# Another order of the first batch's weight rounding and of the weight loads, in a kernel of linear attention and a feed-forward layer

## The chip, the cores and the metric

The kernel runs on one core of one Trainium2 chip. The metric is device microseconds of one execution, median of three. The core has five engines with queues of their own, each strictly in order: PE (matrix products; its weight loads are listed apart as PEld), DVE (vector), ACT (scalar functions), POOL (general) and SP, which here only issues DMA transfers. PE writes into PSUM, of which there are eight banks of 128x512 float32; the rest lies in SBUF.

## The reference

```python
# q, k, v: (8, 8, 576, 64) float32; w_in (512, 2048) and w_out (2048, 512) float64
q_s = exp(q - q.max(-1)); q_s /= q_s.sum(-1) + 1e-9
k_s = exp(k - k.max(2));  k_s /= k_s.sum(2) + 1e-9       # over the sequence
kv = einsum('bhsd,bhse->bhde', k_s, v)
attn = einsum('bhsd,bhde->bhse', q_s, kv)
x = attn.transpose(0, 2, 1, 3).reshape(4608, 512)
out = relu(x @ w_in) ** 2 @ w_out
```

The weights come in 8 bytes per element. The kernel reads them as two 32-bit words and rounds them to float32 itself; float32 numbers are then split into a high and a low part, and each product is made of three (high x high, low x high, high x low).

## The kernel before

**Tiling.** Attention is done per batch and pair of heads: 8 batches of 4 pairs. A pair yields x for 512 of the 576 tokens of its batch in one of four column chunks (`x_hi`, `x_lo`); the other 64 tokens of every batch go to DRAM (`x_left`) and form a ninth block. The feed-forward layer does nine blocks of 512 tokens; in each it makes 16 steps, one per chunk `fc` of 128 hidden columns. A step has a hidden part (`ffn_h`, or `h_part` for the first four: 4 column chunks x 3 matmuls of 128x512, L406 to L408), an activation (`activate`: relu on ACT, square on DVE, `g_hi` on ACT, `g_lo` on POOL or DVE) and, two steps later, an output part (`ffn_out`: 4 x 3 matmuls, L440 to L442), so 24 matmuls a step.

**Weights.** `load_w` fetches a chunk of w_in ("i0" to "i15") or w_out ("o0" to "o15"), 512 KB each, through SP's queue. `split_weight` rounds it: ACT makes a small number of the top byte (L164, here "low word") and scales the upper word into PSUM bank 3 (L166, "bank row"), DVE joins them in two operations (L168, L169, giving `w`), then `finish_split` makes the high part on ACT (L176, a cast) and the low part on POOL (L177). Bank 3 is the only one for this, so ACT's next bank row waits until DVE has made the `w` before it. A low word is ordered behind the last entry of the list `his`.

**Attention of a pair.** `k_max` (DVE maximum, PE transposition L222, DVE `mc`, PE product L250), `k_exp` (`ke`), `q_exp` (DVE row maximum `qm`, POOL subtraction, ACT exp), `q_norm`, `kv` (PE, then `rs` on DVE and `kvn` on DVE or ACT), transposition of q, and the product that gives x (L358), split into `x_hi` (ACT, L188) and `x_lo` (DVE, L189).

**Order.** The program is one long list of instructions; a scheduler lays out each engine's queue by priority and data, units of attention in the first part ranking above the weights' rounding. In the first batch the four pairs run three units apart; behind the fifth unit of each pair one weight chunk is rounded, and behind its eighth the hidden parts of the first four chunks `hs` get this pair's share. After that the steps of block 0 run with attention of batch 1 spread among them in slots (`FIRST_KV`, `EARLY_STEP`, `EARLY_AT`). Two sets of buffers for k, q and v are used in turn, so the third pair's load needs the first pair's tile to be free. At most eight transfers of SP are outstanding. In block 0 the chunks are taken in the order `order0`: 2, 3, 0, 1, 4, 5, ...

Of the kernel before, what the change touches and what calls it, by code (L numbers as in the profile page):

```python
# [8 lines left out]
F32 = mybir.dt.float32  # L9
# [7 lines left out]
P = 128  # L17
# [5 lines left out]
half = slice(0, HALF), slice(HALF, P)  # L23
FLT_MAX = float.fromhex("0x1.fffffep127")
RAWB, WB = 4, 3
EARLY_SPLITS = [("o",2),("o",3),("i",4),("o",0)]
OFFSET = 100
AHEAD = 4
EARLY = 8
PRE = 4  # L30
LOADS = "k0 q0 v0 k1 q1 v1 k2 q2 w0 v2 k3 q3 v3 w1 w2 w3".split()
# [11 lines left out]
def attention_ffn_kernel(ctx: ExitStack, tc: tile.TileContext, q, k, v, w_in, w_out, out):  # L43
# [73 lines left out]
    def load(dst, src, b, pr, n):  # L117
        s = src[b, 2 * pr : 2 * pr + 2]
        lo = s[:, :SPLIT, :].rearrange("h (p j) d -> p h j d", j=LOW)
        hi = s[:, SPLIT:, :].rearrange("h (p j) d -> p h j d", j=HIGH)  # L120
        if n < 2 or b == 0:
            e = nc.scalar if (b, pr, n) in ACT_LOADS else nc.sync
            e.dma_start(dst[:HALF], lo)  # L123
            e.dma_start(dst[HALF:, :, :HIGH, :], hi)
        else:
            for h in range(2):
                nc.sync.dma_start(dst[:HALF, h, :, :D], lo[:, h])
                nc.sync.dma_start(dst[HALF:, h, :HIGH, :D], hi[:, h])

    def tiles(b, pr):  # L130
        i = pr if b == 0 else pr % NB
# [6 lines left out]
        for n in range(3):  # L138
            load_one(b, pr, n)

    chunks, last = [], []

    def load_w(part, fc):
        raw = stay.tile([P, 512, 2], U32, name=f"raw_{part}{fc}", tag=f"{part}{fc}")
# [33 lines left out]

        unsplit.append(parts)

    his, unsplit = [], []

    def finish_split():
        while unsplit:
            unsplit.pop()()

    def split(hi, lo, src):
        nc.scalar.copy(hi, src)  # L188
        nc.vector.tensor_tensor(lo, src, hi.bitcast(F32), op=ALU.subtract)  # L189

    def ordered(f, *args):
# [286 lines left out]
    us = [attention(0, pr) for pr in range(NPAIR)]  # L478
    for u in us:
        u[5], u[6] = u[6], u[5]  # L480
    hs = [banks[i] if i < 2 else ps_first.tile([P, NT], F32, name=f"h_ps{i}", tag="h") for i in range(PRE)]
    for c in LOADS:
        i = int(c[1])
        if c[0] == "w":
            load_w("i", i)
        else:
            load_one(0, i, "kqv".index(c[0]))
    order0 = list(range(2, PRE)) + list(range(min(2, PRE))) + list(range(PRE, NFC))

    def load_more(n):  # L490
        load_w("o", order0[n])
# [5 lines left out]
    for t in range(len(us[0]) + SKEW * (NPAIR - 1)):  # L497
        for pr in range(NPAIR):
            n = t - SKEW * pr
            if 0 <= n < len(us[pr]):  # L500
                with tc.high_priority(OFFSET):
                    us[pr][n]()
                if n == 4:
                    split_weight("i", pr)
                    if pr == NPAIR - 1:
                        for c in EARLY_SPLITS:
                            split_weight(*c)
                if n == 7:
                    finish_split()
                    for fc in range(min(PRE, pr + 1)):  # L510
                        for cc in [pr] if fc < pr else range(pr + 1):
                            h_part(hs[fc], 0, fc, cc)
    start.close()
    ps_o = ctx.enter_context(tc.tile_pool(name="ps_o", bufs=4, space=bass.MemoryType.PSUM))
    late = ctx.enter_context(tc.tile_pool(name="late", bufs=1))
    x_hi.append(late.tile([P, NCC, NT], F32R, name="x_hi1"))
# [1 line left out]

    for pr in range(NB):
        load_pair(1, pr)  # L520
    for n in range(AHEAD, NFC):
        load_more(n)
    steps = [(0, fc) for fc in order0] + [(blk, fc) for blk in range(1, B + 1) for fc in range(NFC)]
    LAG = 2
# [3 lines left out]
    for b in range(1, B):  # L528
        for pr in range(NPAIR):
            if b == 1:  # L530
                base, offs = FIRST_KV + EARLY_STEP * pr, EARLY_AT
            else:
                base, offs = 2 * NFC * (b - 1) + 1 + STEADY_STEP * pr, STEADY_AT
            us = attention(b, pr)
            nxt = b * NPAIR + pr + NB
            if nxt < B * NPAIR:
                i = 5 if b == 1 else 4
                us[i] = lambda f=us[i], nxt=nxt: (f(), load_pair(nxt // NPAIR, nxt % NPAIR))
            for u, o in zip(us, offs):
                slots.setdefault(base + o, []).append(u)  # L540
    for cc, u in enumerate(left_units()):
        slots.setdefault(2 * NFC * (B - 1) + 4 + 6 * cc, []).append(u)


    def in_slot(i):
        for u in slots.get(i, []):
# [60 lines left out]
```

## Time and profile before

| | us |
|---|---|
| median of 3 runs (lowest, highest) | 905.96 (905.91, 908.08) |
| profiled execution, whole | 906.89 |
| its span | 905.0 |
| PE busy | 875.9 (97%) |
| DVE busy | 580.8 (64%) |
| ACT busy | 408.1 (45%) |
| POOL busy | 202.1 (22%) |

The profile is of one execution. Times in it count from the start of the span. Busy PE means that matmuls were in flight, not that it ran at its peak, and the granted clock (1.00 is full) has to be read with it: at half clock PE is just as busy and does half as much. A row of the engines' order of time gives start, duration, engine, line, operation, output and inputs, and in brackets the idle time before it with what ended it. A wait is shown as who waited, for whom, microseconds in total, times, longest.

### The profile page before, as it was taken

To read this page: it belongs to the slowest core of one execution; us is meant where nothing else is said; L and a number is where in the kernel's file an instruction comes from. 1 tells how busy PE (TensorE), PEld (TensorE's weight loads), DVE (VectorE), ACT (ScalarE), POOL (GpSimd) and SP (SyncE) were. 2 spreads that over 40 slices of the span, in tenths; PEclk is the share of its full clock that TensorE was granted. 3 is DMA by queue.
4 is the path that set the end of the run, shared out by engine and by line. 5 is a ranking of instruction groups with operands and counts; after the bars stand their busy time and mean duration, and the time that the engine had idled before them with its cause. 6 is when DMAs were issued, how large, how long until landed. Compare 5 with 4: busy or idle time off the path is not lost.

```text
span 905.0 us, 12673 instructions
## 1 busy us (share of the span) xinstructions
PE 875.9 (97%) x4368; PEld 702.4 (78%) x4368; DVE 580.8 (64%) x1177; ACT 408.1 (45%) x801; POOL 202.1 (22%) x177
## 2 busy tenths in 40 slices
PE   4898989999999999999999999999999999999997
PEld 3576767888878888888888888888888888888885
DVE  6767887887778776878688768876764342222222
ACT  3766756545445443454454444444444232222222
POOL 3666635222213210222122212222222000000000
PEclk9989999999999999999999999999999999999999
DMA  9898211422142223322322123222311030002001
GB/s 234 274 324 246 62 35 54 114 77 82 46 117 71 78 64 89 97 72 71 86 80 81 54 76 96 76 65 65 97 31 32 3 93 1 1 1 46 1 1 46
DMA packets 95743, 73.18 MB, mean 81 GB/s; under 512 B 47552, under 2 KB 85440, under 8 KB 95680
## 3 DMA queue, kind: packets, MB, share of 16 engines
q1 hardware_dynamic: 94944, 71.53, 28.7%
q10 hardware_dynamic: 736, 0.85, 0.4%
q8 instruction: 34, 0.56, 0.2%
q14 instruction: 29, 0.24, 0.1%
HBM read 54.00 MB, written 18.35 MB: 80 GB/s over the span
## 4 chain that ended last, share of the span: by engine, by line
PE 85%; DMA 7%; DVE 4%; SPq 2%; issue 1%; ACT 0%; DVEq 0%
PE bank L406 14%; PE o_ps L440 14%; PE bank L407 14%; PE bank L408 14%; PE o_ps L441 14%; PE o_ps L442 13%; DMA qt<-in_q_dram 4%; DMA raw_i<-in_moe_w_in_dram 3%; PE bank L299 2%; PE bank L378 1%; DMA kt<-in_k_dram 1%; DVE w L169 1%; SPq L149 1%; DVE m L237 1%; SPq L123 0%
## 5 line engine op out<-in xcount | busy, mean ns | idle before, releaser
L406 PE MATMUL bank<-x_hi,wi 128*128 128x512 f32 x568 | 227.6, 401 | 4.3 <-ACT x_hi L188 2.2
L440 PE MATMUL o_ps<-wo,g_hi 128*128 128x512 f32 x576 | 227.5, 397 | 0.8 <-ACT g_hi L419 0.8
L441 PE MATMUL o_ps<-wo,g_hi 128*128 128x512 f32 x576 | 225.7, 392 | 0.0
L407 PE MATMUL bank<-x_lo,wi 128*128 128x512 f32 x568 | 225.6, 397 | 0.0
L408 PE MATMUL bank<-x_hi,wi 128*128 128x512 f32 x568 | 225.2, 396 | 0.0
L442 PE MATMUL o_ps<-wo,g_lo 128*128 128x512 f32 x576 | 224.1, 391 | 0.0
L418 DVE TENSOR_TENSOR r<-r 128x512 f32<-128x512 f32 x128 | 112.0, 875 | 123.3 <-ACT r L412 123.0
L423 DVE TENSOR_TENSOR g_lo<-r,g_hi 128x512 fp32r<-128x512 f32 x132 | 99.3, 752 | 105.8 <-ACT g_hi L419 104.1
L419 ACT CAST g_hi<-r 128x512 fp32r<-128x512 f32 x144 | 89.2, 620 | 129.1 <-PE o_ps L441 77.2
L412 ACT ACTIVATE r<-bank 128x512 f32<-128x512 f32 x142 | 84.5, 596 | 106.1 <-PE bank L408 103.4
L406 PEld LDWEIGHTS bank<-x_hi,wi 128*128 128x128 f32 x568 | 107.6, 190 | 30.9 <-ACT x_hi L188 3.6
L440 PEld LDWEIGHTS o_ps<-wo,g_hi 128*128 128x128 f32 x576 | 108.1, 188 | 25.7 <-ACT g_hi L419 1.0
L408 PEld LDWEIGHTS bank<-x_hi,wi 128*128 128x128 f32 x568 | 107.7, 190 | 24.3
L442 PEld LDWEIGHTS o_ps<-wo,g_lo 128*128 128x128 f32 x576 | 108.1, 188 | 22.9
L441 PEld LDWEIGHTS o_ps<-wo,g_hi 128*128 128x128 f32 x576 | 108.1, 188 | 22.9 <-POOL wo L177 0.2
L407 PEld LDWEIGHTS bank<-x_lo,wi 128*128 128x128 f32 x568 | 107.5, 189 | 22.8 <-issue 0.2
L389 POOL TENSOR_TENSOR x_lo<-xf,x_hi 128x256 fp32r<-128x256 f32 x48 | 39.5, 823 | 378.2 <-ACT x_hi L388 377.4
L332 POOL TENSOR_TENSOR qs<-qT,qs 64x640 fp32r<-64x640 f32 x48 | 81.7, 1703 | 58.7 <-ACT qs L331 50.9
L218 DVE TENSOR_REDUCE m<-kt 128x128 f32<-128x640 f32 x32 | 41.4, 1296 | 18.3 <-DMA kt<-in_k_dram 18.3
L331 ACT CAST qs<-qT 64x640 fp32r<-64x640 f32 x48 | 34.8, 726 | 37.9 <-DMA qT<-bounce 37.4
L380 ACT COPY xf<-bank 64x320 f32<-64x320 f32 (+1 forms) x96 | 37.9, 395 | 22.5 <-PE bank L378 14.3
L265 ACT ACTIVATE qn<-qn 128x640 f32<-128x640 f32 x32 | 23.6, 739 | 53.8 <-DVE qn L262 44.9
(118 smaller groups left out, 775.8 us busy)
## 6 DMA issues: line engine op xcount, KB each, us to landing
out_dram<-o SPq DMA_DIRECT2D x70, 128.0 KB, 2.4
raw_i<-in_moe_w_in_dram SPq DMA_DIRECT2D x16, 512.0 KB, 9.3
raw_o<-in_moe_w_out_dram SPq DMA_DIRECT2D x16, 512.0 KB, 9.0
bounce<-tb SPq DMA_DIRECT2D x24, 320.0 KB, 2.2
qT<-bounce SPq DMA_DIRECT2D x96, 80.0 KB, 2.3
kt<-in_k_dram SPq DMA_DIRECT2D x32, 160.0 KB, 3.0
qt<-in_q_dram SPq DMA_DIRECT2D x30, 160.0 KB, 3.0
vt<-in_v_dram SPq DMA_DIRECT2D x56, 80.0 KB, 2.5
```

The costliest lines, as they stand in the source:

```text
L218: nc.vector.tensor_reduce(m, kk.rearrange("p h j d -> p h d j"), axis=AX.X, op=ALU.max)
L332: nc.gpsimd.tensor_tensor(qs[other], qT[own], qs[own].bitcast(F32), op=ALU.subtract)
L406: nc.tensor.matmul(ps, wi[fc][:, 0, sl], xh[:, cc, :], start=(cc == 0), stop=False)
L407: nc.tensor.matmul(ps, wi[fc][:, 0, sl], xl[:, cc, :], start=False, stop=False)
L408: last.append(nc.tensor.matmul(ps, wi[fc][:, 1, sl], xh[:, cc, :], start=False, stop=(cc == NCC - 1)))
L412: nc.scalar.activation(r, ps, AF.Relu)
L418: nc.vector.tensor_tensor(r, r, r, op=ALU.mult)
L419: gh = nc.scalar.copy(g_hi, r)
L423: e.tensor_tensor(g_lo, r, g_hi.bitcast(F32), op=ALU.subtract)
L440: nc.tensor.matmul(acc[t], g_hi[:, ts], wo[fc][:, 0], start=(n == 0), stop=False)
L441: nc.tensor.matmul(acc[t], g_hi[:, ts], wo[fc][:, 1], start=False, stop=False)
L442: prev = nc.tensor.matmul(acc[t], g_lo[:, ts], wo[fc][:, 0], start=False, stop=(n == NFC - 1))
```

## The change

In the first batch only the first two hidden chunks (`BESIDE = 2`) are rounded and multiplied beside attention, one behind the fifth unit of each of the first two pairs. i2, o0, i3 and o1 are rounded in the program behind the attention of the batch, and the hidden parts of chunks 2 and 3 follow as a whole; a list `start_done` and an entry of each first-batch `x_hi` into `his` order their low words behind the `x_hi` issued last. Before, i2, i3, o2, o3, i4 and o0 were rounded in that stage, the last four in one go behind the fourth pair's kv. The steps of block 0 are taken in plain order 0, 1, 2, ...; the PSUM tiles of the first four hidden parts are swapped to match. Of the weights loaded after the start, o4 to o7 and i8 to i11 are issued behind the loads of batch 1's first two pairs as before; o8 to o11 and i12 to i15 are ordered behind the last v load of the third pair, o12 to o15 behind that of the fourth.

```diff
-EARLY_SPLITS = [("o",2),("o",3),("i",4),("o",0)]
+
+BESIDE = 2
+EARLY_SPLITS = [("i",2),("o",0),("i",3),("o",1)]
 OFFSET = 100
 AHEAD = 4
+
+LATER = 8, 12, 16
...
             for h in range(2):
                 nc.sync.dma_start(dst[:HALF, h, :, :D], lo[:, h])
-                nc.sync.dma_start(dst[HALF:, h, :HIGH, :D], hi[:, h])
+                dmas.append(nc.sync.dma_start(dst[HALF:, h, :HIGH, :D], hi[:, h]))
...
-    chunks, last = [], []
+    chunks, last, dmas = [], [], []
...
-    his, unsplit = [], []
+    his, unsplit, start_done = [], [], []
...
     def split(hi, lo, src):
-        nc.scalar.copy(hi, src)
+        c = nc.scalar.copy(hi, src)
+        if not start_done:
+            his.append(c)
         nc.vector.tensor_tensor(lo, src, hi.bitcast(F32), op=ALU.subtract)
...
-    hs = [banks[i] if i < 2 else ps_first.tile([P, NT], F32, name=f"h_ps{i}", tag="h") for i in range(PRE)]
+    hs = [ps_first.tile([P, NT], F32, name=f"h_ps{i}", tag="h") if i < 2 else banks[i - 2] for i in range(PRE)]
...
-    order0 = list(range(2, PRE)) + list(range(min(2, PRE))) + list(range(PRE, NFC))
+    order0 = list(range(NFC))
...
-                if n == 4:
+                if n == 4 and pr < BESIDE:
                     split_weight("i", pr)
-                    if pr == NPAIR - 1:
-                        for c in EARLY_SPLITS:
-                            split_weight(*c)
                 if n == 7:
                     finish_split()
-                    for fc in range(min(PRE, pr + 1)):
-                        for cc in [pr] if fc < pr else range(pr + 1):
-                            h_part(hs[fc], 0, fc, cc)
+                    for fc in range(BESIDE):
+                        if fc <= pr:
+                            for cc in [pr] if fc < pr else range(pr + 1):
+                                h_part(hs[fc], 0, fc, cc)
+    for c in EARLY_SPLITS:
+        split_weight(*c)
+    finish_split()
+    for fc in range(BESIDE, PRE):
+        for cc in range(NCC):
+            h_part(hs[fc], 0, fc, cc)
     start.close()
+    start_done.append(1)
...
-    for n in range(AHEAD, NFC):
+    for n in range(AHEAD, LATER[0]):
         load_more(n)
...
-                us[i] = lambda f=us[i], nxt=nxt: (f(), load_pair(nxt // NPAIR, nxt % NPAIR))
+                us[i] = lambda f=us[i], nxt=nxt: (f(), load_next(nxt))
...
+    def load_next(nxt):
+        load_pair(nxt // NPAIR, nxt % NPAIR)
+        i = nxt - NPAIR - NB
+        if i + 1 < len(LATER):
+            with tc.issue_after(dmas[-1].ins):
+                for n in range(LATER[i], LATER[i + 1]):
+                    load_more(n)
```

The rows below give an engine's queue. A row has the line, the operation, output<-inputs with buffer numbers and the shape; lines of the change are 4 to 6 higher than those of before (L164 is L168, L166 is L170, L176 is L180, L188 is L192, L224 is L230).

ACT, at the end of the first batch's attention. `raw_` names a weight chunk, `bank3` the bank of the rounding. Before, from the copies of the transposed q of the last two pairs to the last `x_hi`:

```order
L352 COPY qT_91<-bank2_88 128x512
L352 COPY qe_502<-first_ps_503 128x512
L166 ACTIVATE bank3_89<-raw_o3_168 128x512
L176 CAST wo2_473<-w_466 128x512
L164 ACTIVATE raw_i4_166<-raw_i4_166 128x512
L352 COPY qe_502<-first_ps_509 128x64
L352 COPY qT_91<-bank2_88 128x64
L188 CAST x_hi0_75<-first_ps_512 128x512
L166 ACTIVATE bank3_89<-raw_i4_166 128x512
L176 CAST wo3_481<-w_474 128x512
L164 ACTIVATE raw_o0_172<-raw_o0_172 128x512
L188 CAST x_hi0_75<-bank2_88 128x512
```

The same place now, from the last pair's kvn to the next batch's first exp:

```order
L319 ACTIVATE kvn1_85<-first_ps_417,rs_438 64x64 x2
L358 COPY qe_447<-first_ps_454 128x64
L358 COPY qT_91<-bank2_88 128x512
L192 CAST x_hi0_75<-first_ps_457 128x512
L168 ACTIVATE raw_i2_160<-raw_i2_160 128x512
L168 ACTIVATE raw_o0_164<-raw_o0_164 128x512
L358 COPY qT_91<-bank2_88 128x64
L192 CAST x_hi0_75<-bank2_88 128x512
L170 ACTIVATE bank3_89<-raw_o0_164 128x512
L180 CAST wi2_477<-w_472 128x512
L168 ACTIVATE raw_i3_162<-raw_i3_162 128x512
L271 ACTIVATE qn_618<-qn_618 128x640
```

Between the two `x_hi`, and ahead of them, fewer rows of rounding stand; the rows of i2, o0 and i3 follow behind the last `x_hi`.

DVE, at the first key product of batch 1 (`mc` is its maximum, which PE needs ahead of the first output step; `r` is the square of the activation). Before:

```order
L272 TENSOR_REDUCE qs_824<-qn_758 128x10
L224 TENSOR_REDUCE mc_648<-bank2_88 128x1
L416 TENSOR_TENSOR r_610<-r_610,h_ps2_130 128x512
L416 TENSOR_TENSOR r_617<-r_617,h_ps3_131 128x512
L255 TENSOR_TENSOR ke_674<-kt0_78,bank2_88 128x640
L274 RECIPROCAL qs_824<-qs_824 128x10
```

Now:

```order
L422 TENSOR_TENSOR r_626<-r_626,bank0_86 128x512
L280 RECIPROCAL qs_816<-qs_816 128x10
L172 SCALAR_TENSOR_TENSOR bank3_89<-bank3_89,raw_i4_166 128x512
L173 SCALAR_TENSOR_TENSOR w_577<-raw_i4_166,bank3_89 128x512
L172 SCALAR_TENSOR_TENSOR bank3_89<-bank3_89,raw_o2_172 128x512
L230 TENSOR_REDUCE mc_624<-bank2_88 128x1
L173 SCALAR_TENSOR_TENSOR w_583<-raw_o2_172,bank3_89 128x512
L422 TENSOR_TENSOR r_674<-r_674,bank1_87 128x512
L261 TENSOR_TENSOR ke_650<-kt0_78,bank2_88 128x640
L266 TENSOR_REDUCE qm_941<-qt0_82 128x10
```

`mc` stands behind three squares and the rounding of i4 and half of that of o2, where before it stood ahead of the first square, two rows behind the rounding of o0.

SP, the loads of batch 1's third and fourth pair (`qt0`, `kt0`, `vt0`: third pair; `qt1`: fourth). Before:

```order
L123 DMA qt0_82<-in_q_dram 64x2x320
L147 DMA raw_i14_596<-in_moe_w_in_dram 128x4x256
L124 DMA qt0_82<-in_q_dram 64x2x256
L367 DMA x_left_77<-left_499 128x64
L367 DMA x_left_77<-left_541 128x64
L149 DMA raw_o11_598<-in_moe_w_out_dram 128x1024
L147 DMA raw_i15_600<-in_moe_w_in_dram 128x4x256
L149 DMA raw_o12_602<-in_moe_w_out_dram 128x1024
L149 DMA raw_o13_604<-in_moe_w_out_dram 128x1024
L149 DMA raw_o14_606<-in_moe_w_out_dram 128x1024
L149 DMA raw_o15_608<-in_moe_w_out_dram 128x1024
L123 DMA qt1_83<-in_q_dram 64x2x320
```

Now:

```order
L151 DMA raw_i11_568<-in_moe_w_in_dram 128x4x256
L127 DMA qt0_82<-in_q_dram 64x2x320
L128 DMA qt0_82<-in_q_dram 64x2x256
L373 DMA x_left_77<-left_444 128x64
L373 DMA x_left_77<-left_469 128x64
L127 DMA qt1_83<-in_q_dram 64x2x320
L128 DMA qt1_83<-in_q_dram 64x2x256
L127 DMA kt0_78<-in_k_dram 64x2x320
L128 DMA kt0_78<-in_k_dram 64x2x256
L132 DMA vt0_80<-in_v_dram 64x4x64
L131 DMA vt0_80<-in_v_dram 64x5x64 x2
L132 DMA vt0_80<-in_v_dram 64x4x64
```

Both q loads stand directly behind i11, with nothing of o8 and later ahead of them; o8 is the next row behind these, and the fourth pair's k (`kt1`) follows i15.

## The prediction, as written before the run

> **What bounds the kernel now.** I read the page first (engine shares, chain), then the engines by stretch, PE's waits, the chain in order of time, and the engines' rows from 35 to 60 us.
>
> ```profile
> span 905.0 us, 12673 instructions
> PE 85%; DMA 7%; DVE 4%; SPq 2%; issue 1%; ACT 0%; DVEq 0%
> ...
> 55.77:82.40 26.63, 26.63 (x149) 20.58 (x149) 18.66 (x36) 22.00 (x42) 19.39 (x17) 1.00 1.07 332
> 82.60:86.00 3.40, 0.23 (x2) 0.23 (x3) 2.58 (x3) 2.51 (x6) 2.88 (x3) 1.00 0.47 126
> 86.00:89.40 3.40, 3.40 (x10) 2.69 (x10) 3.26 (x5) 0.56 (x1) 0.60 (x1) 0.52 0.60 154
> 96.50:133.10 36.60, 33.07 (x174) 24.25 (x172) 33.89 (x77) 23.24 (x46) 17.29 (x14) 1.00 0.17 44
> 133.10:600.00 466.90, 466.86 (x2375) 378.08 (x2376) 358.27 (x759) 224.36 (x452) 108.06 (x85) 1.00 0.29 79
> ```
>
> After the stretch come its length, then PE, PE's weight loads, DVE, ACT, POOL, the granted clock, DMA share and GB/s. From 133.1 us on PE is never idle and its work is unchanged, so the end moves only as much as PE's place at 133 us moves. Ahead of that there are three stages. Up to 55.77 PE waits for the first x and weights. From 55.77 to 82.40 it is full. Then it stands, runs at half clock, and to 133 us shares the bound with DVE (33.89 of 36.60 us busy), losing 36.60 - 33.07 = 3.5 us.
>
> ```profile
> PE bank L222 <- DVE m L218: 3.3, 1, 3.3
> PE bank L406 <- DVE r L416: 2.1, 3, 1.2
> PE bank L222 <- ACT kvn L313: 0.8, 1, 0.8
> PE bank L299 <- DVE x_lo L189: 0.7, 1, 0.7
> ...
> 60.76 11.31 DMA qt<-in_q_dram
> 73.16 9.88 DMA qt<-in_q_dram
> 83.13 0.62 DVE qm L260
> 84.54 1.18 DVE m L218
> 86.39 0.43 PE bank L407
> 89.98 0.23 PE bank L407
> 91.14 0.04 DVE ke L255
> 93.61 2.82 DMA kt<-in_k_dram
> ```
>
> The longest of PE's waits, 3.3 us, is the key maximum of the second batch's third pair. DVE had queued it behind a row maximum of q (83.13), and that q took 9.88 us to land behind weights of far later steps. The wait also cost clock: a half-rate matmul follows the last after 0.43 us, a full one after 0.23, so 3.4 us at half rate lose 3.4 x 0.20 / 0.43 = 1.6. The stall is worth 3.3 + 1.6 = 4.9 us.
>
> **The change: the later weights.** On SP's queue the two q loads of the third and fourth pair, and the third pair's k, now stand behind i11; o8 to i15 come after the third pair's v, o12 to o15 after the fourth's. Nothing is added: 16 + 16 weight issues before and after. The eight weights that stay ahead of q move 8 x 0.512 = 4.2 MB. At the 332 GB/s of the full stretch that is 12.6 us from their first issue:
>
> ```profile
> 45.97 0.59 SPq L149 DMA_DIRECT2D raw_o<-in_moe_w_out_dram  x1
> ...
> 39.59 1.29 DVE L218 TENSOR_REDUCE m<-kt 128x128 f32<-128x640 f32 x1
> 40.79 0.69 DVE L169 SCALAR_TENSOR_TENSOR w<-raw_o,bank 128x512 uint32<-128x512 uint32 x1
> 41.38 0.82 DVE L260 TENSOR_REDUCE qm<-qt 128x10 f32<-128x640 f32 x1
> 54.14 0.29 DVE L224 TENSOR_REDUCE mc<-bank 128x1 f32<-128x128 f32 x1 [2.44 <-PE bank L222]
> ...
> 54.49 0.49 PE L250 MATMUL bank<-ident,mc 128*128 128x128 f32 x2 [0.38 <-DVE mc L224]
> 55.77 0.47 PE L440 MATMUL o_ps<-wo,g_hi 128*128 128x512 f32 x1 [0.80 <-ACT g_hi L419]
> ```
>
> So q lands near 59 to 61 us, third k (which waits for the first pair's subtraction to free its buffer) near 63, 20 us ahead of PE's need. The stall of 3.3 us and the half clock behind it go: **-4.9**. Late weights: o8 is issued after the second batch's first kv, near 68, and rounded near 85. The fourth pair's k queues behind o8 to i15, 68 + 12.6 = 80.6; DVE reaches it behind the second kv, near 82. Covered, by some 1.5 us: cost nothing.
>
> **The change: rounding in the first batch.** On ACT, between the last pair's kvn and the last x_hi, two of seven rounding rows are left; a low word, two bank rows and two casts are gone:
>
> ```profile
> 48.08 1.26 POOL L262 TENSOR_TENSOR qn<-qt,qm 128x640 f32<-128x640 f32 x1
> 49.75 1.28 POOL L177 TENSOR_TENSOR wo<-w,wo 128x512 fp32r<-128x512 f32 x1
> ...
> 43.14 0.57 ACT L188 CAST x_hi<-bank 128x512 fp32r<-128x512 f32 x1
> ...
> 56.18 0.66 ACT L164 ACTIVATE raw_i<-raw_i 128x512 uint32<-128x512 uint8 x1
> 56.75 0.66 ACT L164 ACTIVATE raw_o<-raw_o 128x512 uint32<-128x512 uint8 x1
> 57.30 0.72 ACT L256 ACTIVATE ke<-ke 128x640 f32<-128x640 f32 x1
> 57.93 1.07 ACT L412 ACTIVATE r<-bank 128x512 f32<-128x512 f32 x2
> 58.89 0.65 ACT L166 ACTIVATE bank<-raw_o 128x512 f32<-128x512 f32 x1
> 59.44 0.63 ACT L176 CAST wi<-w 128x512 fp32r<-128x512 f32 x1
> 59.95 0.64 ACT L419 CAST g_hi<-r 128x512 fp32r<-128x512 f32 x1
> 60.47 0.70 ACT L164 ACTIVATE raw_i<-raw_i 128x512 uint32<-128x512 uint8 x1
> ```
>
> From start to start a low-word row takes 0.57 us, an exp 0.63, a relu 0.48, a bank row 0.55, a cast 0.51. The last x_hi comes 0.57 + 2 x 0.55 + 2 x 0.51 = 2.7 earlier, at 40.4. That is not yet a gain, because of what is late next: i2, o0, i3 and o1. Before, i2, i3 and the first two output chunks were rounded ahead of this x_hi; now they come behind it.
>
> ACT's first bank row of o0 needs i2's w from DVE, which stands behind a key maximum as another w did before (39.59, then 40.79 + 0.69): 41.5. Up to and with i4's bank row ACT then has 6 low words, 4 bank rows, 4 casts, 3 relus, 2 g_hi and 2 exps: 6 x 0.57 + 4 x 0.55 + 4 x 0.51 + 3 x 0.48 + 2 x 0.51 + 2 x 0.63 = 11.4 us. It waits 0.5 for the first exp's input (row maximum 41.38 + 0.82, then POOL 1.3) and 0.9 for r x r, which DVE does behind the fourth key maximum and its sums; with two small copies and the last row's tail it is done at 54.6. In the new DVE order mc of the second batch, which PE multiplies ahead of output step 0, stands behind i4's two DVE rows and o2's first, where before it stood alone (54.14). I take i4's two dependent rows at 2 x 0.69, ACT's o2 bank row 0.65, DVE's first row 0.69, mc 0.29, L250's product 0.49 and 0.1 of hand-overs: 54.6 + 3.6 = **58.2** for step 0 instead of 55.77: **+2.4**. Bounds: 55.5, when PE has done i3's twelve matmuls (on the count above g_hi of step 0 is done at 48.6; POOL then does g_lo, a normalisation and i3's low part, 3 x 1.28, to 52.4; 12 x 0.23), if mc is not late; 59.4 if each of four dependent hand-overs costs 0.3 more. The row of its kind, DVE behind ACT behind DVE, speaks for 58.2. Queued behind the waiting product are 24 matmuls of steps 0 and 1; nobody else waits for it but the first exp of k, due 5.6 us later.
>
> PE's idle time before 58.2 is free by itself, but the clock is not:
>
> ```profile
> 41.66:45.07 3.41, 1.20 (x4) 0.67 (x4) 3.18 (x5) 2.79 (x5) 2.51 (x2) 1.00 0.65 191
> 45.07:48.49 3.42, 2.28 (x6) 1.92 (x7) 3.38 (x6) 1.50 (x4) 1.65 (x2) 0.52 0.71 187
> 48.49:51.90 3.41, 3.41 (x9) 2.64 (x8) 1.49 (x3) 1.82 (x3) 3.25 (x4) 0.50 0.86 291
> ```
>
> After a stretch with 1.20 of 3.41 us busy the clock was halved, and given back only after a full one. In the change PE idles 2.7 us just ahead of step 0. I take half of one such stretch, **+0.8**; bounds 0 and two stretches, 3.2.
>
> The Trainium skill (TensorE: Matmul & The Clock Gate, Why this matters for your kernels) sets the limit at idle gaps over about 3 us; by it 2.7 us would cost nothing and the sum would end 0.4 lower. The trace does not agree: 41.66 to 45.07 held no gap over 2.3 us.
>
> **The sum.** By the end of chunk i7's hidden part (90.3 before): +2.4 + 0.8 - 4.9 = -1.7. Not all of it is kept. There DVE sets the pace: in the new order ke of the third pair follows the rounding of i9 and most of o7's, in which ACT and DVE take turns from PE's key product on (85.77 before; now 58.2 + 0.8 + 26.6 = 85.6): mc 0.4, w 0.7, cast and bank row 1.2, two rows 1.4, bank row 0.65, one row 0.7, hand-overs 0.3: 91.0, before 91.14. The next batch's k load then goes out at once, ahead of a q load that it used to follow (93.61), and lands 1.2 earlier; of this up to 0.6 goes to a rounding row now behind its maximum. DVE is full from there on, so PE leaves 133 us earlier by about **1.0**; the other 0.7 goes into longer waits of the kind listed. Bounds: 0 and the whole 1.7.
>
> Plain order of steps moves no time: the same 24 matmuls a step.
>
> Span 905.0 - 1.0 = 904.0. The profiled execution took 906.89, 1.9 more than its span, and lies 0.9 above the median 905.96; so the median comes to **905.0**.
>
> **The rivals.** (1) *The start is not late:* mc or ACT come through by 55.8. For it: PE's inputs other than mc are there at 55.5. Against: the DVE order. Then the key product and ke behind it come 2.4 earlier too: 1.0 + 2.4 = 3.4, 902.6 (901.3 to 903.5 with the clock's bounds). (2) *Slower, by the clock at step 0:* the idle ahead of step 0 halves the clock for two stretches, as at 45.07 to 51.90: 3.2 instead of 0.8, and start +2.4 to +3.6. It decides once start and clock together cost over 4.9: 5.6 to 6.8, so PE is 0.7 to 1.9 late at 90 us, the DVE stretch begins as much later and has the 0.6 more of the rounding row: 906.7 to 908.5, 907.6. For it: i3's low part, then mc, give two gaps of 1 to 2.8 us in ten. Against: one full stretch lies between. (3) *The late weights become the new wait:* at the 291 GB/s of 48.49 to 51.90 the eight weights take 14.4 us, k lands at 82.4 to 84, DVE stands 1 to 2 us in front of its key product: gain gone, 906. Against: little else moves then (126 to 154 GB/s after 82.6).
>
> **How the numbers follow.** Forecast 905.0 (904 to 906): 0.45. Rival 1: 0.25; rival 2: 0.2; rival 3: 0.1. No change to a measurement is within 0.3%, 2.7 us: 903.2 to 908.7. Faster: most of rival 1 and a fringe of the forecast, 0.29. Slower: the late end of rival 2 with a lost cover on top, 0.13. Same: the rest, 0.58. Range 901.5 to 908.5 leaves out the ends of rivals 1 and 2.
>
> **What would show it.** Right: the q loads land before 62 us; no wait of PE for m over 1 us near 85; step 0 starts at 57.5 to 59 behind mc; the third ke at about 91. Wrong: step 0 by 56 (rival 1), half clock after 58 for over 4 us (rival 2), DVE waiting for k near 82 (rival 3), or PE's 3.5 us of waits before 133 gone, which would mean that DVE does not hold the gain back.

## The result, and the profile after

The changed kernel takes 910.80 us (median of 7 runs, 909.08 to 914.21) against 905.96 before (7 runs, 904.88 to 908.08): ratio 1.0056, 95% interval 1.0035 to 1.0077, slower by half a per cent. Predicted were 905.0, with a range up to 908.5.

The profiled execution took 909.08 us, of which the span is 907.0, 2.0 more than before. It is the fastest of the seven: at a mean granted clock of 0.996 the program took 909.1, at 0.992 909.3 to 911.9, at 0.987 to 0.988 913.8 to 914.2. So the rows below explain 2.0 of the 4.8 us between the medians. Another 1.7 separates this execution from its own median, and 0.9 is how far the profiled execution of before lay above its median. What the 1.7 us consist of is not shown: no trace of another execution of this kernel is on record.

The page of the changed kernel, then its stretches (start and end, length, PE, PE's weight loads, DVE, ACT, POOL, granted clock, DMA share, GB/s):

```profile
span 907.0 us, 12668 instructions
PE 88%; DVE 5%; DMA 4%; SPq 1%; issue 1%; ACT 1%; POOL 0%; DVEq 0%; POOLq 0%; ACTq 0%
```

```profile
84.00:88.00 4.00, 1.74 (x8) 1.04 (x7) 3.73 (x8) 2.49 (x6) 2.39 (x2) 1.00 0.83 223
...
104.00:108.00 4.00, 1.61 (x7) 0.96 (x7) 3.90 (x13) 2.43 (x5) 1.70 (x1) 0.92 0.20 44
108.00:112.00 4.00, 4.00 (x14) 3.16 (x13) 2.38 (x5) 2.01 (x5) 1.29 (x1) 0.66 0.25 74
```

DVE's share of the chain that ended last rose from 4% to 5%. PE stands in two stretches, 84 to 88 and 104 to 108, and behind the second its clock is cut. The same in PE's order of time (lines are 4 to 6 higher than before: L228 is the key product, before L222):

```profile
57.84 0.48 PE L446 MATMUL o_ps<-wo,g_hi 128*128 128x512 f32 x1
...
85.21 0.33 PE L228 MATMUL bank<-ident,m 128*128 128x128 f32 x1
87.80 0.50 PE L412 MATMUL bank<-x_hi,wi 128*128 128x512 f32 x1 [2.26 <-DVE kvn L321]
...
107.29 0.47 PE L228 MATMUL bank<-ident,m 128*128 128x128 f32 x1 [2.39 <-ACT kvn L319]
...
108.41 0.63 PE L448 MATMUL o_ps<-wo,g_lo 128*128 128x512 f32 x1
...
135.06 0.50 PE L412 MATMUL bank<-x_hi,wi 128*128 128x512 f32 x1 [1.16 <-DVE r L422]
```

| PE starts | before | after | later by |
|---|---|---|---|
| output step 0 | 55.77 | 57.84 | 2.1 |
| the matmul behind i7's hidden part | 90.29 | 90.71 | 0.4 |
| fourth pair's key product | 105.51 | 107.29 | 1.8 |
| the next product of mc, 12 matmuls on | 109.08 | 112.23 | 3.2 |
| the last hidden part that had to wait | 133.14 | 135.06 | 1.9 |

The wait for the third pair's m is gone: its product (85.21) starts without one. But PE now waits for kvn, the normalised product of k and v, at both places. It does not read kvn there. The kv product lies in a PSUM bank until kvn has been made of it, and the next hidden part (87.80) and the next key product (107.29) want that bank: in the program, batch 1's attention and the hidden parts of block 0 take three banks in turn.

### The profile page after: what moved, and what is told of

Its sections match the earlier page's. It is cut to its first block, busy times and chain, and to the rows that moved or that the text cites. A ratio compares the mean times of both kernels' runs of the same rounds, so it can differ in the third digit from the quotient of the medians.

```text
span 907.0 us, 12668 instructions
## 1 busy us (share of the span) xinstructions
PE 875.5 (97%) x4368; PEld 702.1 (77%) x4368; DVE 582.1 (64%) x1177; ACT 408.5 (45%) x801; POOL 202.0 (22%) x177
## 4 chain that ended last, share of the span: by engine, by line
PE 88%; DVE 5%; DMA 4%; SPq 1%; issue 1%; ACT 1%; POOL 0%; DVEq 0%; POOLq 0%; ACTq 0%
PE o_ps L446 14%; PE bank L412 14%; PE o_ps L447 14%; PE o_ps L448 14%; PE bank L414 13%; PE bank L413 13%; PE bank L305 2%; DMA kt<-in_k_dram 2%; PE bank L384 1%; DMA raw_i<-in_moe_w_in_dram 1%; DVE m L224 1%; DVE w L173 1%; DVE bank L172 1%; DVE m L243 1%; PE first_ps L305 1%
## 5 line engine op out<-in xcount | busy, mean ns | idle before, releaser
L414 PEld LDWEIGHTS bank<-x_hi,wi 128*128 128x128 f32 x568 | 107.1, 189 | 25.6 <-POOL wi L181 1.3
L413 PEld LDWEIGHTS bank<-x_lo,wi 128*128 128x128 f32 x568 | 107.1, 189 | 22.6 <-issue 0.2
L224 DVE TENSOR_REDUCE m<-kt 128x128 f32<-128x640 f32 x32 | 41.4, 1298 | 18.3 <-DMA kt<-in_k_dram 18.3
```

The costliest lines, as they stand in the source:

```text
L224: nc.vector.tensor_reduce(m, kk.rearrange("p h j d -> p h d j"), axis=AX.X, op=ALU.max)
L413: nc.tensor.matmul(ps, wi[fc][:, 0, sl], xl[:, cc, :], start=False, stop=False)
L414: last.append(nc.tensor.matmul(ps, wi[fc][:, 1, sl], xh[:, cc, :], start=False, stop=(cc == NCC - 1)))
```

## The experiments

Pairs are counted through the batches: 4 to 7 are batch 1's, 8 is the next batch's first. All ratios are to the kernel before, with 95% intervals. The last two columns are PE's longest wait at each place in the profiled execution; "half" means that half clock followed it.

| kernel | ratio | near 85 to 90 | near 100 to 110 |
|---|---|---|---|
| before | 1 | 3.32 for m, half | 0.78 for kvn |
| the change | 1.0056 (1.0035 to 1.0077) | 2.26 for kvn | 2.39 for kvn, half |
| a_start_only | 1.0012 (1.0002 to 1.0022) | 2.87 for kvn, half | 1.18 for kvn |
| b_loads_only | 1.0054 (1.0037 to 1.0070) | 2.91 for kvn | 3.36 for kvn, half |
| e_after_kvn | 1.0043 (1.0028 to 1.0057) | 2.42 for kvn | 1.18 for kvn |
| n_first_order | 1.0008 (1.0000 to 1.0017) | none | 1.73 for x_lo |
| c_after_reduce | 1.0012 (0.9999 to 1.0025) | 3.04 for kvn, half | 0.35 for kvn |
| d_before_reduce | 0.9974 (0.9964 to 0.9983) | 2.50 for m, half | 0.44 for r |
| f2_after_order | 1.0018 (1.0006 to 1.0029) | none | 1.81 for r |
| h_after_order_reduce | 0.9986 (0.9975 to 0.9997) | none | 1.51 for x_lo |
| i_loads_order_reduce | 0.9979 (0.9971 to 0.9988) | 0.88 for ke | 1.01 for x_lo |
| p_order_m8 | 0.9995 (0.9986 to 1.0004) | none | 1.96 for x_lo, half |
| r_order_last_loads | 0.9950 (0.9938 to 0.9962) | none | 0.57 for kvn |
| u_i_m8_last | 0.9948 (0.9935 to 0.9962) | 0.71 for ke | 1.0 for r |
| w_order_last_loads_copies | 0.9996 (0.9987 to 1.0006) | none | 1.8 for r |

### Which part of the change

`a_start_only`: the changed kernel, later weights loaded as before.

```diff
-LATER = 8, 12, 16
+LATER = 16,
```

> The changed kernel with the loads of all later weights put back to where they were before (behind the first two pairs' loads of batch 1); rounding in the first batch and plain order as changed. Theory 1 (the loss is made by the late loads, through the order that they give DVE): step 0 still comes at about 58.1, 2.3 late, but the wait for the third pair's m, which a q load sets at about 85, takes most of it in (about 1 us left of 3.3), and there is no wait for kvn over 1 us at 87 or at 107: 904.5 to 907.5, ratio 0.9985 to 1.0015. Theory 2 (the late start makes the loss, and the late loads gain): the 2.3 us come on top of the old waits, ratio 1.0025 or more, and at least the 1.0056 of the changed kernel if the late loads gained anything.

`b_loads_only`: the kernel before with `LATER = 8, 12, 16`, `load_next` and its list `dmas` from the change, nothing else.

> The kernel before, with only the loads of the later weights moved as in the change; rounding and order of steps as before. Theory 1: the wait of 3.3 us for the third pair's m at 85.77 goes, but the fourth pair's m and its late k now stand in front of the second pair's kvn on DVE, and PE waits 1.5 us or more for kvn near 85 to 88; little or nothing of the gain is left, ratio 0.9975 to 1.004. Theory 2 (the prediction's terms, without the late start): PE is 4.9 us earlier at 90 us, of which 1 to 3.4 reach the end: 902.6 to 905, ratio 0.9963 to 0.9985, and no wait for kvn over 1 us.

The start alone gives 1.0012, the loads alone 1.0054, as much as the whole change. So the late loads make the loss, and the 2.1 us of a later start hardly reach the end. That half of theory 1 held. Its other half did not: the start alone, too, has a wait of 2.87 for kvn at 87.92, where I had expected none over 1 us; there a key maximum (84.70) and a row sum (85.98) stand between rs (84.04) and kvn (87.29) on DVE. The loads alone came out above both theories (at most 1.004): the first wait is there, as theory 1 had it, but a second one of 3.36, which I had not expected, follows. In order of time:

```profile
82.73 1.30 DVE L219 TENSOR_REDUCE m<-kt 128x128 f32<-128x640 f32 x1 [2.26 <-DMA kt<-in_k_dram]
...
86.06 0.47 PE L407 MATMUL bank<-x_hi,wi 128*128 128x512 f32 x1 [2.91 <-DVE kvn L316]
...
106.91 0.33 PE L223 MATMUL bank<-ident,m 128*128 128x128 f32 x1 [3.36 <-ACT kvn L314]
```

### The first wait: what stands between rs and kvn on DVE

DVE of the changed kernel from the second pair's rs (the sum from which its kvn is made) to that kvn:

```profile
83.03 0.15 DVE L313 TENSOR_SCALAR rs<-bank 128x1 f32<-128x1 f32 x1
83.77 1.32 DVE L224 TENSOR_REDUCE m<-kt 128x128 f32<-128x640 f32 x1 [0.59 <-DMA kt<-in_k_dram]
85.01 0.80 DVE L266 TENSOR_REDUCE qm<-qt 128x10 f32<-128x640 f32 x1
85.73 0.69 DVE L172 SCALAR_TENSOR_TENSOR bank<-bank,raw_o 128x512 uint32<-128x512 uint32 x1
86.33 0.14 DVE L314 RECIPROCAL rs<-rs 128x1 f32<-128x1 f32 x1
86.39 0.27 DVE L230 TENSOR_REDUCE mc<-bank 128x1 f32<-128x128 f32 x1
86.58 0.67 DVE L173 SCALAR_TENSOR_TENSOR w<-raw_o,bank 128x512 uint32<-128x512 uint32 x1
87.18 0.57 DVE L321 TENSOR_SCALAR kvn<-bank,rs 64x64 f32<-64x64 f32 x2
```

The chain itself is 0.15 + 0.14 + 0.57 = 0.9 us long; it took 4.7. Between its parts stand m of the fourth pair (0.59 of waiting for the late k, then 1.32) and qm of pair 8. Both belong to the moved loads, and no one needs them yet. Before, the same chain was done at 81.70, and PE ran out of work only at 82.45, so the bank was free in time and the change made this wait:

```profile
80.27 0.15 DVE L307 TENSOR_SCALAR rs<-bank 128x1 f32<-128x1 f32 x1
80.93 0.16 DVE L308 RECIPROCAL rs<-rs 128x1 f32<-128x1 f32 x1
81.12 0.58 DVE L315 TENSOR_SCALAR kvn<-bank,rs 64x64 f32<-64x64 f32 x2
```

`e_after_kvn`: the fourth pair's m behind the second pair's kvn.

```diff
+    def first_of(n, f):
+        with ExitStack() as order:
+            if n == 7: order.enter_context(tc.issue_after(kvns[5].ins))
+            f()
-            nc.vector.tensor_reduce(m, kk.rearrange("p h j d -> p h d j"), axis=AX.X, op=ALU.max)
+            first_of(n, lambda: nc.vector.tensor_reduce(m, kk.rearrange("p h j d -> p h d j"), axis=AX.X, op=ALU.max))
```

> The changed kernel, with the key maximum m of batch 1's fourth pair ordered behind the second pair's kvn on DVE. Theory 1 (the wait of 2.26 at 87.8 comes from m and its wait for the late k standing between rs and kvn): kvn comes at about 85.0 to 85.9 instead of 87.18, PE's wait for it falls to 0.6 or less, the hidden part of i7 ends 1.6 to 2.2 earlier (88.6 to 89.1). What of it reaches the end depends on the stretch to 133, where DVE is full: 0 to 2 us, ratio to before 1.0033 to 1.0056. Theory 2 (kvn is late because of PE's kv or the rounding rows before it): the wait stays over 1.5.

The wait did not go (2.42). The next moved load took the place of the first; its qm now stood behind rs and waited for a q:

```profile
83.02 0.15 DVE L317 TENSOR_SCALAR rs<-bank 128x1 f32<-128x1 f32 x1
85.18 0.82 DVE L270 TENSOR_REDUCE qm<-qt 128x10 f32<-128x640 f32 x1 [2.02 <-DMA qt<-in_q_dram]
```

`n_first_order`: both behind kvn.

```diff
+    def behind(x):
+        return tc.issue_after(x.ins) if x else ExitStack()
...
+            with behind(n == 7 and kvns[5]):
                 nc.vector.tensor_reduce(m, kk.rearrange("p h j d -> p h d j"), axis=AX.X, op=ALU.max)
...
+            with behind(n == 8 and kvns[5]):
                 nc.vector.tensor_reduce(qm, qq, axis=AX.X, op=ALU.max)
```

> The changed kernel with DVE's order set at the first place only: the fourth pair's m and the next batch's first qm behind the second pair's kvn; the copies stay ahead of the third pair's rs. Both theories: PE's wait for the second pair's kvn (2.26 at 87.8) under 0.5, the hidden part of i7 done near 89 instead of 91. If each of the two waits reaches the end by itself, about half of the 0.38% between the changed kernel (1.0056) and the order at both places (1.0018) comes back: ratio 1.003 to 1.0045, and PE still waits 1 to 2.4 for the third pair's kvn near 105. If the DVE stretch behind it takes in what the first place gains, the ratio stays at 1.0045 to 1.006 and the wait near 105 grows by what was gained.

PE does not stand there any more, and the ratio falls to 1.0008, further than either theory gave. This shows the cause of the first wait. From output step 0 (59.01) to the matmul behind i7's hidden part (88.61) PE now takes 29.6 us, where before it took 34.5 (55.77 to 90.29): 4.9 less, the size of the prediction's term. The whole gain of 0.48% is 4.3 us, more than the wait of 2.26; what makes up the rest is not shown. Near 105 the wait for kvn is 1.17; new is one for x_lo, to which I come back below.

### The second wait: DVE's copies and POOL

The third pair's rs comes at 103.83 before, at 105.50 in the change, though the next batch's key maximum ahead of it starts earlier (95.85, before 96.52). What lies between has grown by 2.3 us: 0.9 more for the four copies, the rest a rounding row more and three small maxima that now come ahead of rs. DVE and POOL in order of time, first before, then the change:

```profile
99.86 1.29 POOL L177 TENSOR_TENSOR wi<-w,wi 128x512 fp32r<-128x512 f32 x1
101.93 1.77 DVE L237 COPY m<-m 32x4 f32<-32x4 f32 x4
102.20 1.29 POOL L423 TENSOR_TENSOR g_lo<-r,g_hi 128x512 fp32r<-128x512 f32 x1 [1.04 <-ACT g_hi L419]
103.83 0.14 DVE L307 TENSOR_SCALAR rs<-bank 128x1 f32<-128x1 f32 x1
```

```profile
100.65 1.29 POOL L181 TENSOR_TENSOR wi<-w,wi 128x512 fp32r<-128x512 f32 x1 [1.22 <-ACT wi L180]
100.85 2.53 DVE L243 COPY m<-m 32x4 f32<-32x4 f32 x3
101.89 1.29 POOL L429 TENSOR_TENSOR g_lo<-r,g_hi 128x512 fp32r<-128x512 f32 x1
104.76 0.69 DVE L173 SCALAR_TENSOR_TENSOR w<-raw_o,bank 128x512 uint32<-128x512 uint32 x1
105.50 0.15 DVE L313 TENSOR_SCALAR rs<-bank 128x1 f32<-128x1 f32 x1
```

Three copies of 32x4 elements took 2.53 us and ended 0.2 behind POOL's two operations; before, POOL paused from 101.15 to 102.20.

`c_after_reduce`: the changed kernel, with these copies written as maxima over one element. The values and the order of DVE, PE, POOL and SP stay the same.

```diff
-                    nc.vector.tensor_copy(m4[:, g], m1[g * BLK : (g + 1) * BLK])
+                    nc.vector.tensor_reduce(m4[:, g], m1[g * BLK : (g + 1) * BLK].rearrange("p (c o) -> p c o", o=1), axis=AX.X, op=ALU.max)
```

> The changed kernel, with the four small DVE copies of the cross-partition maximum (L243, 32x4) written as DVE maxima over one element; order on PE, DVE, POOL and SP unchanged. Theory 1 (the copies wait for POOL): in the changed kernel three of them took 2.53 us at 100.85 while POOL was busy without a break from 100.65 to 103.18; as maxima they take about 0.16 each, so the third pair's rs moves from 105.50 to about 103.5, its kvn from 106.62 to about 104.7, PE's wait for it falls from 2.39 to under 0.7 and the half clock behind it goes: PE passes the 105 to 112 stretch 2 to 3 us earlier, and 1 to 3 us of that reach the end (DVE also gets some 1.3 to 2.5 us back at 122 to 133): ratio to before 1.0025 to 1.0045 instead of 1.0056. Theory 2 (the copies are long for a reason of their own, or the rounding rows ahead of rs in DVE's queue set its time): the maxima are as long, or rs stays at 105 to 105.5; PE's wait at 107 stays over 2 and the ratio at 1.0056.

```profile
105.67 1.29 POOL L181 TENSOR_TENSOR wi<-w,wi 128x512 fp32r<-128x512 f32 x1 [1.22 <-ACT wi L180]
105.86 0.47 DVE L243 TENSOR_REDUCE m<-m 32x4 f32<-32x4 f32 x3
106.92 1.29 POOL L429 TENSOR_TENSOR g_lo<-r,g_hi 128x512 fp32r<-128x512 f32 x1
110.24 0.33 PE L228 MATMUL bank<-ident,m 128*128 128x128 f32 x1 [0.35 <-ACT kvn L319]
```

POOL is as busy there as in the change, the three take 0.47, and PE's wait is 0.35 instead of 2.39. PE reaches the place as long after the next batch's m as in the change (9.0 us in both), so it is DVE that comes earlier. The ratio falls from 1.0056 to 1.0012, further than expected, although the first wait was longer in this execution (3.04, its k having landed late).

`d_before_reduce`: the same edit in the kernel before.

> The kernel before, with the four small DVE copies of the cross-partition maximum (L237) written as DVE maxima over one element; order unchanged. Before 133 us the three groups of copies take 1.77, 1.76 and 1.30 us there, POOL being busy in each; as maxima 0.6 each, so DVE gets about 3 us back in a stretch in which it is full and PE waits 3.5 us. Theory 1 (PE's waits there follow DVE's total work): 1 to 3 us reach the end, ratio 0.9967 to 0.999. Theory 2 (the waits are latencies of single chains): ratio 0.999 to 1.0005.

0.9974, a value of theory 1: the copies cost the old kernel 0.26% too. Two edits went further along this line. `k_reduce_glow` has g_lo of the last four chunks of block 0 on POOL:

```diff
-G_LOW_POOL = 12
+G_LOW_POOL = 16
```

> The kernel before, with the copies as maxima and g_lo of the last four chunks of block 0 on POOL (1.29 us each there) instead of DVE (0.76 each). If DVE's total work before PE is full still sets PE's place at 133 us, up to 3 us less of it: ratio 0.995 to 0.997. If these four come too late to matter (PE is full behind 130), the same as the maxima alone, 0.997 to 0.998.

`l_reduce_all` writes the last copy of that chain (`mt`) as a maximum too:

```diff
-                nc.vector.tensor_copy(mt, m5.broadcast_to([P, 4, BLK]))
+                nc.vector.tensor_reduce(mt, m5.rearrange("p c (o u) -> p c o u", u=1).broadcast_to([P, 4, BLK, 1]), axis=AX.X, op=ALU.max)
```

> The kernel before, with the copies as maxima and the one remaining copy of that chain (mt, 128x128, L244: 0.21 to 0.88 us) as a maximum too. If it waited for POOL like the small ones, the 0.88 falls to the 0.2 to 0.3 of the undisturbed ones and up to 0.7 us of DVE time comes back: ratio 0.9967 to 0.9975; if its work rules, no difference to 0.9974.

They gave 0.9975 (0.9966 to 0.9984) and 0.9973 (0.9963 to 0.9983): no difference. The copy `mt` did fall to 0.27 to 0.29 us; the four g_lo come at 131 to 153 us, too late to matter.

### Both waits together

`f2_after_order`: the order of `n_first_order`, and the copies of pair 8 behind the third pair's rs and reciprocal (`recs[6]`).

```diff
+                with behind(n == 8 and recs[6]):
                     for g in range(4):
                         nc.vector.tensor_copy(m4[:, g], m1[g * BLK : (g + 1) * BLK])
```

> The changed kernel, with DVE's order set at two places: the fourth pair's m and the next batch's first qm (the data of the late loads) behind the second pair's kvn, and the copies L243 of the next batch's first maximum behind the third pair's rs and its reciprocal. Theory 1 (both waits of PE for kvn come from DVE's order): kvn of the second pair near 85.3, PE's wait of 2.26 at 87.8 falls under 0.5; rs of the third pair near 103, PE's wait of 2.39 at 107.3 under 0.5 and no half clock behind it; the change then gives what the prediction's terms gave, 0.9975 to 1.0005. Theory 2 (DVE's total work in the stretch sets the end): the waits come back under other names by 133 us, ratio 1.0015 to 1.0045.

`h_after_order_reduce`: this order, and the maxima (the line of `c_after_reduce` inside this block).

> The run before this one (order at two places), and the copies written as maxima. Both waits for kvn under 0.5; the copies, which then stand behind rs, no longer delay it, so against the order alone only DVE's time counts: 1 to 3 us less DVE work before 133. Theory 1 (single chains): 0 to 0.5 us faster than the order alone; theory 2 (DVE's total): 1 to 2.5 us faster than the order alone. Ratio to before 0.9955 to 0.9995.

`i_loads_order_reduce`: the kernel before with the late loads, this order and the maxima, so without the late start: the diffs of `b_loads_only`, `f2_after_order` and `c_after_reduce` in one.

> The kernel before with the late loads, DVE's order at the two places and the maxima, but the old rounding and order of steps, so that step 0 is not late. Against the run before this one it has the start of before, 55 to 56 instead of 58.1: if a late start reaches the end, 1 to 2.3 us faster than that run, ratio 0.994 to 0.998; if the stretch to 133 takes it in, the same as that run.

Order alone gives 1.0018, theory 2's value: rs comes early, but the copies behind it met POOL again, and PE waited for the r queued behind them:

```profile
102.48 0.15 DVE L319 TENSOR_SCALAR rs<-bank 128x1 f32<-128x1 f32 x1
102.74 2.96 DVE L248 COPY m<-m 32x4 f32<-32x4 f32 x4
109.82 0.66 PE L359 MATMUL bank<-ident,qn 128*128 128x128 f32 x4 [1.81 <-DVE r L428]
```

With the maxima it is 0.9986, 0.32% below the order alone and so beyond the 2.5 us of theory 2. The gains don't add up: mending the first place alone, or the copies alone, brings 0.44 to 0.48%, both 0.70%. The early start of `i_loads_order_reduce` brings 0.07% more, inside the intervals. `m_loads_order_glow`, that kernel with `G_LOW_POOL = 16`, gave 0.9973 (0.9962 to 0.9983), not told apart from it:

> The kernel before with the late loads, the order at two places, the maxima, and g_lo of the last four chunks on POOL. If DVE's total work is what takes in the earlier start and the missing stalls (0.9979 without this edit), up to 3 us come out: ratio 0.9945 to 0.997, the fastest of all; else 0.9975 to 0.9985.

### Where the rest of the gain goes: the next k behind the last weights

At i7's hidden part `n_first_order` is 1.7 us early (88.61, before 90.29), as the prediction had it, and yet its span is no shorter (905.1). Its rows show where the gain went, DVE first:

```profile
97.04 1.30 DVE L228 TENSOR_REDUCE m<-kt 128x128 f32<-128x640 f32 x1 [3.83 <-DMA kt<-in_k_dram]
99.86 0.67 DVE L195 TENSOR_TENSOR x_lo<-bank,x_hi 128x512 fp32r<-128x512 f32 x1
100.59 0.87 PE L311 MATMUL bank<-vt,ke 128*64 128x65 f32 x20 [1.73 <-DVE x_lo L195]
```

DVE stands 3.83 us in front of pair 8's k, and rounding rows and x_lo queue behind. That k is issued behind o12 to o15. Two edits of `h_after_order_reduce` attack this from two sides. `p_order_m8` moves the waiting m behind rs on DVE:

```diff
-            with behind(n == 7 and kvns[5]):
+            with behind(n == 7 and kvns[5] or n == 8 and recs[6]):
```

> h_after_order_reduce, with also the next batch's first key maximum m (the one that waits for k at 96.75) behind the third pair's rs on DVE. If DVE's stand of 3.62 us in front of that k is what takes in the rest of the gain, the x_lo that PE waits 1.51 us for comes 2 us or more earlier (99.57 to under 97.5), PE's waits near 100 to 105 (1.51, 0.51, 0.58) fall under 1 in sum, ratio 0.9955 to 0.9975. If DVE's total work to 133 us sets the end, the work only changes places: 0.998 to 0.999, as without the edit (0.9986).

`r_order_last_loads` issues o12 to o15 behind pair 8's loads:

```diff
-LATER = 8, 12, 16
+LATER = 8, 12, 12, 16
```

> h_after_order_reduce, with o12 to o15 loaded behind the next batch's first pair instead of ahead of it. If the late weights delay that k, it lands 3 us after its issue instead of 4.9 (near 95.0 instead of 96.75), DVE's stand in front of it falls from 3.62 to about 2, PE's wait for x_lo from 1.51 to under 0.5: ratio 0.9970 to 0.9982 against 0.9986. If the time of that k does not matter, 0.998 to 0.999.

In this kernel the loads were it: 0.9950 against 0.9986, more than the 0.9970 to 0.9982 expected. In `h_after_order_reduce`, then in this kernel, the issue of k on SP's queue, m and x_lo:

```profile
91.21 0.61 SPq L127 DMA_DIRECT2D kt<-in_k_dram  x1
96.75 1.31 DVE L228 TENSOR_REDUCE m<-kt 128x128 f32<-128x640 f32 x1 [3.62 <-DMA kt<-in_k_dram]
99.57 0.67 DVE L195 TENSOR_TENSOR x_lo<-bank,x_hi 128x512 fp32r<-128x512 f32 x1
```

```profile
91.02 0.61 SPq L127 DMA_DIRECT2D kt<-in_k_dram  x1
94.74 1.33 DVE L228 TENSOR_REDUCE m<-kt 128x128 f32<-128x640 f32 x1 [1.61 <-DMA kt<-in_k_dram]
97.59 0.67 DVE L195 TENSOR_TENSOR x_lo<-bank,x_hi 128x512 fp32r<-128x512 f32 x1
```

k lands 2.0 us sooner after nearly the same issue, x_lo follows it, and PE's wait for x_lo is gone. Moving m instead made it worse (0.9995): behind it stood a qm, whose q came later still:

```profile
98.94 0.82 DVE L272 TENSOR_REDUCE qm<-qt 128x10 f32<-128x640 f32 x1 [5.18 <-DMA qt<-in_q_dram]
```

`u_i_m8_last` is `i_loads_order_reduce` (the old start) with both of these edits; `v_d_m8` is `d_before_reduce` with pair 8's m and its maxima behind rs (`with behind(n == 8 and recs[6])` around both), without late loads:

> i_loads_order_reduce (the old rounding and start, late loads, order at two places, maxima; 0.9979) with both edits of the two runs before this one. If the DVE stands are the rest of the loss: 0.994 to 0.9965, the fastest of all; if DVE's total work rules, 0.997 to 0.998.

> The kernel before with the maxima (0.9974) and the next batch's first m behind the third pair's rs; no late loads. DVE stands only 1.36 us in front of that k here: if such stands matter, 0.5 to 1.4 us faster than the maxima alone, 0.996 to 0.997; else 0.997 to 0.998.

They gave 0.9948 and 0.9966 (0.9954 to 0.9979). The first is level with `r_order_last_loads`, but differs from it in the place of m as well as in the start; the second is not told apart from the maxima alone. `w_order_last_loads_copies` is `f2_after_order` with `LATER = 8, 12, 12, 16`, so the change with order and last loads mended and its copies left:

> The changed kernel with DVE's order at the two places and o12 to o15 loaded behind the next batch's first pair; copies as they were. If these three are the whole of what the prediction missed, and its other terms hold (start 2.4 late, stall of 4.9 gone), the ratio is 0.9975 to 0.9995 (0.999 predicted), 0.25 to 0.4% below the order alone (1.0018). If the late weights only cost together with the maxima, 1.001 to 1.002.

0.9996, 0.22% below the order alone and so a little short of what was expected: the prediction's 0.999 lies in its interval, and so does no gain at all. `t_i_last_loads`, meant to be the fastest (`i_loads_order_reduce` with `LATER = 8, 12, 12, 16`), was a miss:

> The kernel before with late loads, order at two places, maxima and o12 to o15 behind the next batch's first pair: the same as r_order_last_loads (0.9950) but for the start, which is 2.3 us earlier here. If PE's place at 133 us still follows its start, 1 to 2.3 us faster, 0.9925 to 0.994; if DVE's total work takes it in, 0.994 to 0.9955.

1.0001 (0.9992 to 1.0010), against 0.9979 without that edit, and against 0.9950 of `r_order_last_loads`, from which it differs by the start alone. So what the last loads bring with the new start they do not bring with the old one. Here DVE waited for a q that came behind the moved weights (in `r_order_last_loads` only 0.20 us for the same qm), and the rounding behind it was late later on:

```profile
113.81 0.82 DVE L267 TENSOR_REDUCE qm<-qt 128x10 f32<-128x640 f32 x1 [2.33 <-DMA qt<-in_q_dram]
130.29 0.50 PE L413 MATMUL bank<-x_hi,wi 128*128 128x512 f32 x1 [1.44 <-ACT wi L177]
```

Half clock followed (granted 0.58 from 132 to 136 us; 1.00 without that edit). These rows are a reading; no run separates them. The fastest kernels, 902.06 and 901.72 us in runs where the kernel before took 906.06, beat both.

## Why the prediction was wrong, step by step

**Rounding in the first batch: right.** The last x_hi came at 40.70 (predicted 40.4), and step 0 behind mc (57.26, then L256) at 57.84 (58.2). The clock, for which I had put 0.8 us, cost nearly nothing in this execution: it was 0.98 from 56 to 60 us. But in the profiled executions of three kernels with the same start (`c_after_reduce`, `p_order_m8`, `w_order_last_loads_copies`) PE waited 2.45 to 2.47 us for mc there, and the next six to eight matmuls came 0.43 us apart instead of 0.23. That is 1.2 to 1.6 us, rival 2's mechanism at half its price. In `c_after_reduce`:

```profile
58.23 0.52 PE L256 MATMUL bank<-ident,mc 128*128 128x128 f32 x2 [2.47 <-DVE mc L230]
...
59.40 0.63 PE L448 MATMUL o_ps<-wo,g_lo 128*128 128x512 f32 x1
```

That a late start is mostly taken in later held in one pair, `i_loads_order_reduce` and `h_after_order_reduce`: step 0 at 54.63 and 57.74, ratios level. It is no rule: `t_i_last_loads`, with the early start, is 0.5% slower than `r_order_last_loads`.

**The stall for m: right that it goes and what it is worth, wrong that nothing takes its place.** The q loads were there at 61.83 and the product at 85.21 did not wait; with the first wait mended (`n_first_order`) the 4.9 us came out up to here. I asked when the fourth pair's k would land and whether PE would wait for *its* product; I did not ask what stood behind that m on DVE. It was the row that frees PE's next bank: kvn ended at 81.70 before and began at 87.18 after. So at 90.7 PE was 0.4 late, where I had 1.7 early.

**Late weights "cost nothing": this is the step that failed.** The late loads alone made the kernel 0.54% slower. The eight weights ahead of k are 8 x 0.524 = 4.2 MB (the sum wrote 0.512), so k was to land at 80.6, 1.5 us ahead of DVE; DVE got it at 83.77 and had waited 0.59. Rival 3 named this wait (82.4 to 84) but looked for it at the wrong victim, the key product, and so priced it at 906. I also covered o8 to i15 only. The last four weights, ahead of pair 8's k, appear in the sum solely as a k that goes out at once. With the order and the maxima mended, moving them behind that k brings 0.36% (0.9986 to 0.9950); with the old start it costs 0.22% (0.9979 to 1.0001), so their price holds for this kernel only.

**"DVE is full from there on, so 1.0 comes through": half right.** The next k did land earlier (DVE's m at 95.85, before 96.52), and the third ke at 91.56 was within 0.6 of the 91.0. What I took from this, that PE follows DVE's amount of work, is only part of it. Shorter copies paid in the old kernel too (0.9974), but in the change DVE was busy no longer than before: 62.4 us of the stretch from 56 to 133 us before, 61.8 after. Which of its rows came first, and which of them met POOL, put PE 3.2 us late at 112.23, 1.4 of it half clock (12 matmuls took 4.4 us, before 3.0). Of that 1.3 were given back by 133 us.

**The forecast.** With the order at both places and the last loads mended the change takes 0.9996 of the time before (0.9987 to 1.0006). That fits the 905.0, but also no gain, so it does not show that every term had its size; the two that were measured by themselves, the start (2.1 for 2.4) and the stall (4.9), had. What was missing were waits in places that I had priced at nothing: for kvn behind the late k and q, for kvn behind copies that met POOL, and for x_lo behind the last weights.

## What to carry to other kernels

When a load is moved, follow the instruction that waits for it on its in-order engine, and ask what is queued behind that instruction and who waits for *that*: a reduction 20 us early for its own user held up a chain of 0.9 us that PE needed. Before a stall's removal is counted as a gain, ask what else will stand there: here the small DVE row that frees PE's next bank had been in time before, and the change itself made it late. And before deciding that an engine is full, see whether its small instructions last as long as their size says.

## What the runs showed of the hardware

**Small DVE copies are held up while POOL works.** A copy of 32x4 takes 0.15 us alone (four took 0.66 in `n_first_order`, with POOL idle) and up to 1.26 against a POOL operation of 1.29; a maximum of the same shape takes 0.16 in either case. The Trainium skill (SBUF — State Buffer, Who interferes with whom) has the rule: a DVE copy can take the ports that it shares with GpSimd, whoever is first holds them for the whole instruction, and a reduction never contends on trn2. The trace agrees in the copies and maxima shown above.

**The length of a gap does not decide the clock.** Gaps of 2.31 (`l_reduce_all`), 2.39 and 2.50 us were followed by half clock, gaps of 2.26, 2.42 and 2.91 were not. In the changed kernel the half rate ended at 110.5; counted back in steps of 3.41 us, the length of the stretches quoted in the prediction, the gap of 2.39 lies within one step (103.7 to 107.1) with 1.2 us of matmuls in it, and the gap of 2.26 is shared by two (83.2 to 86.7 and 86.7 to 90.1) with 2.3 us each. The Trainium skill (TensorE: Matmul & The Clock Gate, Why this matters for your kernels) puts the limit at gaps over about 3 us; the trace does not agree, since three gaps of 2.3 to 2.5 us were enough. The rows fit a clock set by fixed stretches, but no run varied a gap's place alone.
